# Strassen's scheme in the first MLP product of chunks 2 to 8 (three of four column groups), with in-place result sums and a new placement of attention

## The chip, the cores and the metric

The kernel runs on one core of a Trainium2 chip. The metric is the device time of one execution in microseconds (us). Times before and after are medians of several executions of the same rounds.

Engine names in the profile: PE is TensorE (matrix products), PEld its weight loads, DVE is VectorE, ACT is ScalarE, POOL is GpSimd, SP is the engine that issues most DMAs. PSUM holds the results of this kernel's matmuls, in buffers of two kinds, `ring` and `ops`; SBUF holds its other tiles.

## The reference

```python
def _attn_ref(q, k, v):                     # (8 batches, 8 heads, 576 positions, 64)
    q_s = np.exp(q - np.max(q, axis=-1, keepdims=True))
    q_s = q_s / (np.sum(q_s, axis=-1, keepdims=True) + 1e-09)
    k_s = np.exp(k - np.max(k, axis=2, keepdims=True))
    k_s = k_s / (np.sum(k_s, axis=2, keepdims=True) + 1e-09)
    kv = np.einsum('bhsd,bhse->bhde', k_s, v)
    return np.einsum('bhsd,bhde->bhse', q_s, kv)

def _moe_ref(x, w_in, w_out):               # x: 4608 x 512, w_in: 512 x 2048, w_out: 2048 x 512
    h = x @ w_in
    g = h * (1.0 / (1.0 + np.exp(-h)))      # SiLU
    return g @ w_out
# x is the attention output, heads side by side; result 4608 x 512, float32
```

## The kernel before

The 4608 rows are worked in nine chunks of 512 rows (0 to 8; the first product takes 576 of them in chunk 0 and 448 in chunk 1). A chunk has a first product (`mm1`, 512 x 512 by 512 x 2048), a SiLU on ScalarE, and a second product (2048 x 512), which runs interleaved with the first product of the next chunk. While chunk t is worked, the attention of batch t+1 is prepared: two exponentials on ScalarE, the row sums on VectorE, the scaling by their reciprocals and the cast of v on GpSimd (VectorE for batch 1), a transposing DMA, and two small products. In the timelines here, each engine executes its operations in the order in which the program issues them (one example, below: in chunk 4 of the changed kernel two sums run from 169.16 us on, ahead of an add at 172.68; in e1, which only issues those sums later, the add runs at 163.33 us and the sums behind it, at 169.01 and 171.00); the whole argument below turns on that order.

The second product of chunks 2 to 8 uses Strassen's scheme (Winograd's form): the matrix is halved in both directions, and seven products of quarters replace eight. The price is sums: `presum` builds the sums of activations on VectorE, and `after` combines the products from PSUM, also on VectorE. The first product is plain.

```python
def mm1(t, fb):                              # first product, one block of 128 columns
    for off, size in part[t]:
        hps = ps.tile([128, TCH], FP32, name="hps", tag="ring", bufs=PSB["ring"])
        for c in range(NC):                  # NC = 4: four matmuls of 512 moving columns
            nc.tensor.matmul(out=hps[:, 0:size], lhsT=W1[:, c, fb * 128:(fb + 1) * 128],
                             rhs=XT[t][:, c, off:off + size], start=(c == 0), stop=(c == NC - 1))
        # ... cut ...
            nc.scalar.activation(out=GT[g][:, fb, col:col + n], in_=hps[:, h], func=ACT.Silu)

def presum(t, i, f):                         # sums for the second product, f = half of the blocks
    S1, S2, S4 = SW[t % 2]
    V = nc.vector
    if i == 0:
        V.tensor_add(S1[:, f], quad(t, 0, f, 1), quad(t, 1, f, 1))
    elif i == 1:
        V.tensor_sub(S2[:, f], S1[:, f], quad(t, 0, f, 0))
    elif i == 2:
        V.tensor_sub(quad(t, 0, f, 1), quad(t, 0, f, 0), quad(t, 0, f, 1))
    else:
        V.tensor_sub(S4[:, f], quad(t, 1, f, 0), S2[:, f])

def plan_attn(b, u, sm, vs, tp, ks, ox, eng=nc.gpsimd):   # where attention of batch b stands
    for i, (x, y) in enumerate((("qt", "eq"), ("kt", "ek"))):
        plan(u + sm[i], lambda x=x, y=y: [exp(b, x, y, cc) for cc in range(2)])
    for cc in range(2):
        plan(u + sm[0] + 2 + 2 * cc, lambda cc=cc: (qsum(b, cc), qnorm(b, cc, nc.gpsimd)))
        plan(u + vs[cc], lambda cc=cc: vcast(b, cc, eng))
    plan(u + tp, lambda: tr_dma(b, nc.sync))
    # ... cut: loads of the next batch, the two small products ...
```

The softmax here doesn't subtract the row's maximum and nothing guards it: scores larger than these inputs give would overflow.

## Time and profile before

| | before |
|---|---|
| median time | 294.33 us (292.29 to 295.12, 4 runs) |
| span of the profiled run | 290.7 us |
| TensorE busy | 263.8 us (91%) |
| VectorE / ScalarE / GpSimd busy | 115.7 (40%) / 178.0 (61%) / 54.9 (19%) |

The first part of the page gives the busy time of each engine; the row "PEclk" of the second part gives the TensorE clock that was granted, in tenths of full speed, in 40 equal slices. Two lines of the page of before:

```profile
PE 263.8 (91%) x2269; PEld 162.4 (56%) x2306; DVE 115.7 (40%) x217; ACT 178.0 (61%) x287; POOL 54.9 (19%) x44
PEclk9999999999999999999999999999999999999999
```

TensorE bounds the kernel, and in this profiled run its clock does not fall (in later calls, runs of this kernel have mean clocks of 0.983 to 0.994). Of the view of TensorE's waits, the first two lines (total us, times, longest us): the copy `s` on ScalarE holds TensorE up four times, once in each of chunks 3 to 6.

```profile
PE ops L273 <- ACT s L295: 6.6, 4, 1.8
PE hps L206 <- ACT GT L220: 3.2, 2, 1.9
```

In TensorE's timeline of before (start, duration, line, operation, tiles, count; in brackets the idle time before it and what ended that), the wait of chunk 5 looks like this, and it is the only one above 0.3 us in its chunk:

```profile
169.66 1.03 PE L206 MATMUL hps<-XT,W 128*128 128x512 bf16 x4
172.27 1.03 PE L273 MATMUL ops<-W,GT 128*128 128x256 bf16 x8 [1.59 <-ACT s L295]
```

Chunk 0, where batch 1's inputs arrive: ScalarE's and SP's timelines of before.

```profile
30.23 0.88 ACT L220 ACTIVATE GT<-hps 128x320 bf16<-128x320 f32 x3 [0.96 <-PE hps L206]
31.82 1.28 ACT L91 ACT_TABLE_LOAD   x1 [0.70 <-DMA qt<-in_q_dram]
```

```profile
40.36 4.59 SPq L122 DMA_TRANSPOSE qT<-eq  x1
45.14 0.43 SPq L82 DMA_DIRECT2D qt<-in_q_dram  x1
```

The exponential waits only 0.70 us for its load, and the transposing DMA is issued ahead of the loads of the next batch. The second place is one that I read too late: VectorE's and GpSimd's timelines of before, in chunk 5.

```profile
175.63 0.69 DVE L231 TENSOR_TENSOR SW<-GT 128x1024 bf16<-128x1024 bf16 x1 [2.69 <-ACT GT L220]
176.36 1.52 DVE L233 TENSOR_TENSOR SW<-SW,GT 128x1024 bf16<-128x1024 bf16 x1
```

```profile
175.71 1.63 POOL L98 CAST vaug<-vt 128x1152 bf16<-128x1152 f32 x1
```

Two operations of the same shape take 0.69 and 1.52 us. The first began 0.08 us ahead of the GpSimd cast and kept its length, while the cast took 1.63 us instead of 1.16; the second began inside the cast and ended 0.54 us after it. Here nothing waits for it.

### The profile page before, as it was taken

To read this page: it belongs to the slowest core of one execution; us is meant where nothing else is said; L and a number is where in the kernel's file an instruction comes from. 1 tells how busy PE (TensorE), PEld (TensorE's weight loads), DVE (VectorE), ACT (ScalarE), POOL (GpSimd) and SP (SyncE) were. 2 spreads that over 40 slices of the span, in tenths; PEclk is the share of its full clock that TensorE was granted. 3 is DMA by queue.
4 is the path that set the end of the run, shared out by engine and by line. 5 is a ranking of instruction groups with operands and counts; after the bars stand their busy time and mean duration, and the time that the engine had idled before them with its cause. 6 is when DMAs were issued, how large, how long until landed. Compare 5 with 4: busy or idle time off the path is not lost.

```text
span 290.7 us, 5481 instructions
## 1 busy us (share of the span) xinstructions
PE 263.8 (91%) x2269; PEld 162.4 (56%) x2306; DVE 115.7 (40%) x217; ACT 178.0 (61%) x287; POOL 54.9 (19%) x44
## 2 busy tenths in 40 slices
PE   8589879995998997999799979997999999999993
PEld 3356544442443464656566656665656665665882
DVE  3830233841044335624562456245624041431621
ACT  4685794698797779356945594559545445544100
POOL 0661050035062007200630054004400000000000
PEclk9999999999999999999999999999999999999999
DMA  7799999966709920696049804971333012201234
GB/s 256 248 202 273 304 289 272 392 202 120 288 0 257 388 70 2 122 359 234 3 102 323 283 11 89 322 267 41 84 72 72 2 36 56 54 1 38 60 87 108
DMA packets 42377, 46.43 MB, mean 160 GB/s; under 512 B 18544, under 2 KB 29808, under 8 KB 42352
## 3 DMA queue, kind: packets, MB, share of 16 engines
q1 hardware_dynamic: 37312, 38.35, 44.1%
q0 software_dynamic: 5040, 7.73, 11.9%
q8 instruction: 18, 0.29, 0.4%
q14 instruction: 7, 0.06, 0.1%
HBM read 36.70 MB, written 9.44 MB: 159 GB/s over the span
## 4 chain that ended last, share of the span: by engine, by line
PE 54%; ACT 20%; DMA 18%; issue 3%; SPq 2%; POOL 2%; DVE 0%; ACTq 0%
PE ops L273 24%; PE hps L206 23%; DMA qt<-in_q_dram 8%; DMA out_dram<-oq 7%; ACT ek L91 5%; ACT L91 4%; ACT eq L91 4%; PE ops L331 3%; DMA vt<-in_v_dram 3%; ACT L220 3%; ACT GT L220 3%; PE kvps L153 2%; PE o L187 2%; SPq L122 1%; ACT s L295 1%
## 5 line engine op out<-in xcount | busy, mean ns | idle before, releaser
L206 PE MATMUL hps<-XT,W 128*128 128x512 bf16 (+3 forms) x612 | 139.2, 357 | 5.4 <-ACT GT L220 3.2
L220 ACT ACTIVATE GT<-hps 128x512 bf16<-128x512 f32 (+2 forms) x176 | 86.2, 523 | 77.3 <-PE hps L206 65.5
L206 PEld LDWEIGHTS <-W 128*128 128x128 bf16 x640 | 61.9, 98 | 52.4 <-issue 5.9
L111 POOL TENSOR_TENSOR eq<-eq,rzq 128x1152 bf16<-128x1152 bf16 x14 | 29.5, 2118 | 138.5 <-DVE rzq L106 138.5
L273 PEld LDWEIGHTS <-GT 128*128 128x128 bf16 x448 | 43.4, 98 | 22.0 <-issue 8.5
L105 DVE TENSOR_REDUCE zq<-eq 128x18 f32<-128x1152 bf16 x16 | 21.3, 1331 | 48.9 <-ACT eq L91 48.7
L273 PEld LDWEIGHTS <-SW 128*128 128x128 bf16 x336 | 31.9, 98 | 9.4 <-issue 0.8
L273 PE MATMUL ops<-W,GT 128*128 128x256 bf16 x224 | 28.7, 272 | 6.6 <-ACT s L295 6.6
L331 PE MATMUL ops<-W,GT 128*128 128x512 bf16 x120 | 31.5, 379 | 0.6 <-issue 0.2
L273 PE MATMUL ops<-TW,GT 128*128 128x256 bf16 x224 | 28.6, 273 | 0.4
L273 PE MATMUL ops<-TW,SW 128*128 128x256 bf16 x224 | 28.8, 273 | 0.0
L290 DVE SCALAR_TENSOR_TENSOR oq<-ops,u 128x512 f32<-128x512 f32 x14 | 9.7, 691 | 32.5 <-PE ops L273 32.5
L198 ACT CAST XT<-o 128x512 bf16<-128x512 f32 (+3 forms) x36 | 18.3, 564 | 5.1 <-PE o L187 5.1
L231 DVE TENSOR_TENSOR SW<-GT 128x1024 bf16<-128x1024 bf16 x14 | 9.6, 689 | 27.1 <-ACT GT L220 27.1
L91 ACT ACTIVATE eq<-qt 128x1152 bf16<-128x1152 f32 x16 | 17.9, 1157 | 3.0 <-DMA qt<-in_q_dram 2.9
L290 DVE SCALAR_TENSOR_TENSOR u<-ops,s 128x512 f32<-128x512 f32 x14 | 9.7, 692 | 23.4 <-PE ops L273 21.8
L331 PEld LDWEIGHTS <-GT 128*128 128x128 bf16 x128 | 12.1, 98 | 12.1 <-issue 0.7
L91 ACT ACTIVATE ek<-kt 128x1152 bf16<-128x1152 f32 x16 | 17.8, 1153 | 1.5 <-DMA kt<-in_k_dram 1.5
L98 POOL CAST vaug<-vt 128x1152 bf16<-128x1152 f32 x12 | 15.7, 1317 | 0.0
L220 ACT ACT_TABLE_LOAD x11 | 14.1, 1283 | 0.2
L273 PE MATMUL ops<-W,SW 128*128 128x256 bf16 x112 | 14.2, 273 | 0.0
L153 PE MATMUL kvps<-vaug,ek 64*64 64x65 bf16 x576 | 8.1, 194 | 6.4 <-ACT GT L220 2.8
(45 smaller groups left out, 140.9 us busy)
## 6 DMA issues: line engine op xcount, KB each, us to landing
qt<-in_q_dram SPq DMA_DIRECT2D x6, 1152.0 KB, 6.5
kt<-in_k_dram SPq DMA_DIRECT2D x6, 1152.0 KB, 9.4
vt<-in_v_dram SPq DMA_DIRECT2D x6, 1152.0 KB, 11.8
out_dram<-oq SPq DMA_DIRECT2D x42, 128.0 KB, 2.9
out_dram<-oq SPq DMA_DIRECT2D x60, 64.0 KB, 2.1
W<-in_moe_w_in_dram POOLq DMA_DIRECT2D x4, 512.0 KB, 9.9
W<-in_moe_w_out_dram POOLq DMA_DIRECT2D x4, 512.0 KB, 17.5
qt<-in_q_dram SPq DMA_DIRECT2D x2, 576.0 KB, 4.3
```

Source lines behind the costliest of these rows:

```text
L91: nc.scalar.activation(out=o, in_=jgd(st[b][src], cc), func=ACT.Exp)
L98: eng.tensor_copy(o, jgd(st[b]["vt"], cc))
L105: nc.vector.reduce_sum(out=st[b]["zq"][:, cc], in_=e, axis=AX.X)
L111: eng.tensor_tensor(out=e, in0=e, in1=r[:, :, :, None].to_broadcast([128, J, 2, D]), op=ALU.mult)
L153: nc.tensor.matmul(out=t[r][g * 64:(g + 1) * 64, 0:E1], lhsT=st[b]["ek"][r * P:(r + 1) * P, j, G * D:(G + 1) * D], rhs=vaug[b % 2][r * P:( ...
L198: nc.scalar.copy(out=x, in_=o1[g][:, 0:size])
L206: nc.tensor.matmul(out=hps[:, 0:size], lhsT=W1[:, c, fb * 128:(fb + 1) * 128], rhs=XT[t][:, c, off:off + size], start=(c == 0), stop=(c == ...
L220: nc.scalar.activation(out=GT[g][:, fb, col:col + n], in_=hps[:, h], func=ACT.Silu)
L231: V.tensor_add(S1[:, f], quad(t, 0, f, 1), quad(t, 1, f, 1))
L273: nc.tensor.matmul(out=o[:, a, :], lhsT=l(f), rhs=r(f), start=bool(first and a == 0 and f == 0), stop=(f == HF - 1), skip_group_check=True,)
L290: nc.vector.scalar_tensor_tensor(out=out, in0=o, scalar=1.0, in1=x, op0=ALU.mult, op1=ALU.add)
L331: nc.tensor.matmul(out=OP[t, tb], lhsT=GT[t][:, fc, tb * 128:(tb + 1) * 128], rhs=W2[:, fc, :], start=(fc == 0), stop=(fc == NFB - 1),)
```

## The change

The intent: the first product of chunks 2 to 8 gets the same scheme in three of its four groups of column blocks (group 0 stays plain, to give VectorE time to make the sums of the input). Seven products of 4 matmuls of 256 columns replace what were 16 matmuls of 512 columns per group. Results are summed in place to save buffers; PSUM is split 6 + 2 instead of 5 + 3; `vaug`, the tile for q and the sums SW become single-buffered; the positions of attention, of the sums and of the second product's pieces are written out anew for each chunk. The core of the diff, with lines left out:

```diff
-    vaug = [glob.tile([128, J, NG * E1], BF16, name=f"vaug{i}") for i in range(2)]
+    vaug = glob.tile([128, J, NG * E1], BF16, name="vaug")
-    LDB = {"qt": 2, "kt": 1, "vt": 1}
+    LDB = {"qt": 1, "kt": 1, "vt": 1}
+    def xsum(t, i):          # four sums of the chunk's input, VectorE
+    def vsum(i, k):          # eight sums of W1, VectorE, once
+    def product1(t, g, k):   # product k of group g: 2 x 2 matmuls of 256 columns, then
+        if k == 1:           # a copy s1 (ScalarE, for group 1 VectorE)
+        elif k == 6:
+            add(new("u2"), MP[t, g, "s1"])
+        elif k == 7:
+            add(new("u3"), MP[t, g, "s1"])
+        elif k == 2:
+            silu(o, 0, 0)
+        else:
+            x = MP[t, g, {5: "u3", 4: "s1", 3: "u2"}[k]]
+            add(x, x)                        # VectorE, from PSUM, in place
+            silu(x, *{5: (1, 1), 4: (1, 0), 3: (0, 1)}[k])
-    PSB = {"ring": 5, "ops": 3}
+    PSB = {"ring": 6, "ops": 2}
  ... cut ...
+    POS = {1: 0, 6: 1, 2: 3, 7: 4, 5: 5, 4: 6, 3: 9}     # order of the seven products in a group
+    def plan_attn(b, t, sm, qs, vs, tp, ks, ox, lq, lkv, eng=nc.gpsimd):
+        # sm: exponentials; qs: sums of q; vs: casts of v; tp: transpose;
+        # ks, ox: small products; lq, lkv: loads of the next batch. The loads of a position
+        # are now issued ahead of a transpose of the same position.
-    plan_attn(1, begin[1], (-18, -11), (-6, -5), -11, (-4, -3), (-2, 0), V)
+    plan_attn(1, 0, (6, 12), (8, 9), (11, 12), 12, (13, 14), (15, 16), 12, None, V)
+    plan_attn(2, 1, (5, 9), (7, 8), (9, 10), 10, (12, 13), (14, 15), 9, 11)
+    plan_attn(3, 2, (4, 8), (6, 8), (10, 12), 11, (16, 18), (21, 23), 10, 13)
     for b in range(4, B):
-        plan_attn(b, begin[b], (-25, -25), (-23, -21), -14, (-11, -9), (-5, -3))
+        plan_attn(b, b - 1, (1, 1), (4, 6), (6, 8), 10, (13, 16), (19, 21), 11, 12)
+            pre((t + 1, 6), 3, 0)            # the two sums S4 of the second product
+            pre((t + 1, 7), 3, 1)
```

More of the change, by code (lines that the diff above doesn't have):

```diff
@@ L54 @@
     TW = [glob.tile([128, HF, HM], BF16, name=f"TW{i}") for i in range(4)]
-    SW = [
-        [glob.tile([128, HF, 2, 128], BF16, name=f"SW{i}_{j}") for i in range(3)]
-        for j in range(2)
-    ]
-    vaug = [glob.tile([128, J, NG * E1], BF16, name=f"vaug{i}") for i in range(2)]
+    SW = [glob.tile([128, HF, 2, 128], BF16, name=f"SW{i}") for i in range(3)]
+    HT = TCH // 2
+    HK = NC // 2
+    F0 = 2
+    TX = [glob.tile([128, HK, (HF - F0) * 128], BF16, name=f"TX{i}") for i in range(4)]
+    XS = [glob.tile([128, HK, HT], BF16, name=f"XS{i}") for i in range(4)]
+    vaug = glob.tile([128, J, NG * E1], BF16, name="vaug")
     kvn = [glob.tile([128, 2, 2, D], BF16, name=f"kvn{i}") for i in range(3)]
@@ L93, in vcast @@
     def vcast(b, cc, eng):
-        o = vaug[b % 2].rearrange("p j (g e) -> p j g e", e=E1)[:, :, 2 * cc:2 * cc + 2, 0:D]
+        o = vaug.rearrange("p j (g e) -> p j g e", e=E1)[:, :, 2 * cc:2 * cc + 2, 0:D]
         if eng is nc.scalar:
@@ L155, in kv @@
                         lhsT=st[b]["ek"][r * P:(r + 1) * P, j, G * D:(G + 1) * D],
-                        rhs=vaug[b % 2][r * P:(r + 1) * P, j, G * E1:(G + 1) * E1],
+                        rhs=vaug[r * P:(r + 1) * P, j, G * E1:(G + 1) * E1],
                         start=(j == 0),
@@ L221, in mm1 @@
                 a += n
+    MP = {}
+    def xsum(t, i):
+        A = [[XT[t][:, k * HK:(k + 1) * HK, r * HT:(r + 1) * HT] for k in range(2)] for r in range(2)]
+        S1, S2, S3, S4 = XS
+        V = nc.vector
+        if i == 0:
+            V.tensor_add(S1, A[1][0], A[1][1])
+        elif i == 1:
+            V.tensor_sub(S2, S1, A[0][0])
+        elif i == 2:
+            V.tensor_sub(S3, A[0][0], A[1][0])
+        else:
+            V.tensor_sub(S4, A[0][1], S2)
+    def vsum(i, k):
+        c = lambda n: slice(n * HF * 128 + F0 * 128, (n + 1) * HF * 128)
+        B = [[W1[:, h * HK + k, c(n)] for n in range(2)] for h in range(2)]
+        T1, T2, T3, T4 = TX
+        o, a, b = (
+            (T1, B[0][1], B[0][0]),
+            (T2, B[1][1], T1[:, k]),
+            (T3, B[1][1], B[0][1]),
+            (T4, B[1][0], T2[:, k]),
+        )[i]
+        nc.vector.tensor_sub(o[:, k], a, b)
@@ new lines, in product1, with new, add, silu @@
+    def product1(t, g, k):
+        S1, S2, S3, S4 = XS
+        T1, T2, T3, T4 = TX
+        A = lambda r, h: (lambda c: XT[t][:, h * HK + c, r * HT:(r + 1) * HT])
+        S = lambda x: (lambda c: x[:, c, :])
+        B = lambda h, n: (
+            lambda c, f: W1[:, h * HK + c, (n * HF + f) * 128:(n * HF + f + 1) * 128]
+        )
+        T = lambda x: (lambda c, f: x[:, c, (f - F0) * 128:(f - F0 + 1) * 128])
+        bank, first, l, r = {
+            1: ("A", 1, B(0, 0), A(0, 0)),
+            2: ("A", 0, B(1, 0), A(0, 1)),
+            6: ("B", 1, T(T2), S(S2)),
+            7: ("B", 0, T(T3), S(S3)),
+            4: ("B", 0, T(T4), A(1, 1)),
+            5: ("C", 1, T(T1), S(S1)),
+            3: ("C", 0, B(1, 1), S(S4)),
+        }[k]
+        if first:
+            MP[t, g, bank] = ps.tile([128, 2, HT], FP32, name="hps", tag="ring", bufs=PSB["ring"])
+        o = MP[t, g, bank]
+        for f in range(2):
+            for c in range(HK):
+                nc.tensor.matmul(
+                    out=o[:, f, :],
+                    lhsT=l(c, 2 * g + f),
+                    rhs=r(c),
+                    start=bool(first and f == 0 and c == 0),
+                    stop=(c == HK - 1),
+                    skip_group_check=True,
+                )
+        def new(name):
+            MP[t, g, name] = mp.tile([128, 2, HT], FP32, name=name, tag="mt", bufs=6)
+            return MP[t, g, name]
+        def add(out, x):
+            nc.vector.scalar_tensor_tensor(
+                out=out, in0=o, scalar=1.0, in1=x, op0=ALU.mult, op1=ALU.add
+            )
+        def silu(x, r, n):
+            if t not in GT:
+                GT[t] = mp.tile([128, NFB, TCH], BF16, name="GT")
+            y = GT[t][:, n * HF + 2 * g:n * HF + 2 * g + 2, r * HT:(r + 1) * HT]
+            nc.scalar.activation(out=y, in_=x, func=ACT.Silu)
+        if k == 1:
+            if g in COPY_V:
+                nc.vector.tensor_scalar_mul(out=new("s1"), in0=o, scalar1=1.0)
+            else:
+                nc.scalar.activation(out=new("s1"), in_=o, func=ACT.Copy, scale=1.0)
+        elif k == 6:
[4 more added lines that the diff above has]
+            silu(o, 0, 0)
+        else:
+            x = MP[t, g, {5: "u3", 4: "s1", 3: "u2"}[k]]
+            add(x, x)
+            silu(x, *{5: (1, 1), 4: (1, 0), 3: (0, 1)}[k])
@@ L223, in quad @@
+    COPY_V = (1,)
     def quad(t, h, f, r):
@@ L227, in presum @@
     def presum(t, i, f):
-        S1, S2, S4 = SW[t % 2]
+        S1, S2, S4 = SW
         V = nc.vector
@@ L253, in product @@
     def product(t, k, a):
-        S1, S2, S4 = SW[t % 2]
+        S1, S2, S4 = SW
         T1, T2, T3, T4 = TW
@@ L284, in after, with new @@
     def after(t, k, o):
-        def new(name, bufs=1):
-            WP[t, name] = mp.tile([128, 2, HM], FP32, name=name, bufs=bufs)
+        def new(name):
+            WP[t, name] = mp.tile([128, 2, HM], FP32, name=name, tag="oq", bufs=6)
             return WP[t, name]
@@ L300, in after @@
         else:
-            q = new("oq", 4)
             if k == 2:
+                q = new("c11")
                 nc.scalar.activation(out=q, in_=o, func=ACT.Copy, scale=1.0)
             else:
-                add(q, WP[t, {5: "u3", 4: "s1", 3: "u2"}[k]])
+                q = WP[t, {5: "u3", 4: "s1", 3: "u2"}[k]]
+                add(q, q)
             qstore(t, q, *{2: (0, 0), 5: (1, 1), 4: (1, 0), 3: (0, 1)}[k])
@@ L326, in mm2 @@
         if qd == 0:
-            tag = "ops" if tb < 3 else "ring"
+            tag = "ops" if tb < 2 else "ring"
             OP[t, tb] = ps.tile([128, DM], FP32, name="ops", tag=tag, bufs=PSB[tag])
@@ L341, in store @@
     def store(t, tb, dve=0):
-        ost = mp.tile([128, DM], FP32, name="oq", bufs=4)
+        ost = mp.tile([128, DM], FP32, name="oq", tag="oq", bufs=6)
         if dve:
@@ L364 @@
     nc.vector.tensor_copy(ident, ident_f)
-    for t in vaug:
-        nc.vector.memset(t.rearrange("p j (g e) -> p (j g) e", e=E1)[:, :, D:E1], 1.0)
+    nc.vector.memset(vaug.rearrange("p j (g e) -> p (j g) e", e=E1)[:, :, D:E1], 1.0)
     FQ = DFF // 4
@@ L429, with xlist @@
     ORDER = (1, 6, 2, 7, 5, 4, 3)
-    xs = []
-    for t in range(NCH):
-        for i in range(NFB):
-            fb = i if t < STD else (i % 2) * HF + i // 2
-            xs.append((("mm1", t), lambda t=t, fb=fb: mm1(t, fb)))
-    behind = [[] for _ in range(len(xs) + 1)]
-    def trail(x, key, f):
-        behind[min(max(x, 0), len(xs) - 1)].append((key, f))
+    POS = {1: 0, 6: 1, 2: 3, 7: 4, 5: 5, 4: 6, 3: 9}
+    HALVES = [(m, a) for m in ORDER for a in range(2)]
+    def xlist(t):
+        if t < STD:
+            return [lambda fb=fb: mm1(t, fb) for fb in range(NFB)]
+        n = [lambda fb=fb: mm1(t, fb) for fb in (0, HF, 1, HF + 1)]
+        p = sorted((7 * g + POS[m], g, m) for g in range(1, HF // 2) for m in ORDER)
+        return n + [lambda g=g, m=m: product1(t, g, m) for _, g, m in p]
@@ L440, with trail @@
+    X = [xlist(t) for t in range(NCH)]
+    behind = {}
+    def trail(t, i, f):
+        behind.setdefault((t, i), []).append(f)
     for i in range(NFB):
-        trail(min(5 + i, NFB - 1), ("mm2", 0), lambda i=i: mm2(0, i))
+        trail(0, min(5 + i, NFB - 1), lambda i=i: mm2(0, i))
+    late = (0, 2, 4, 6, 9, 12, 15, 18, 21)
     for i in range(NFB):
-        trail(NFB + 6 + i * 3 // 2, ("mm2", 1), lambda i=i: mm2(1, i))
-    for t in range(STD, NCH):
-        for i, (m, a) in enumerate((m, a) for m in ORDER for a in range(2)):
-            late = 3 if t == NCH - 2 and i > 6 else 0
-            trail((t + 1) * NFB + 2 + i + late, ("mm2", t), lambda t=t, m=m, a=a: product(t, m, a))
@@ L448 @@
-    units = []
-    for i, x in enumerate(xs):
-        units.append(x)
-        units.extend(behind[i])
-    begin = {t: next(u for u, f in enumerate(units) if f[0] == ("mm1", t)) for t in range(NCH)}
-    index = [u for u, f in enumerate(units) if f[0][0] == "mm1"]
-    at = [[] for _ in units]
-    def plan(u, f):
-        at[u].append(f)
-    def plan_attn(b, u, sm, vs, tp, ks, ox, eng=nc.gpsimd):
+        if i < NFB - len(late):
+            trail(1, 6 + i * 3 // 2, lambda i=i: mm2(1, i))
+        else:
+            trail(2, late[i - NFB + len(late)], lambda i=i: mm2(1, i))
@@ new lines, with plan @@
+    YAT = (2, 3, 5, 7, 9, 11, 13, 15, 17, 19, 21, 23, 23, 23)
+    for t in range(STD, NCH - 1):
+        for i, (m, a) in enumerate(HALVES):
+            x = len(X[t + 1]) - 1 if t == NCH - 2 and i > 10 else YAT[i]
+            trail(t + 1, x, lambda t=t, m=m, a=a: product(t, m, a))
+    for m, a in HALVES:
+        X[NCH - 1].append(lambda m=m, a=a: product(NCH - 1, m, a))
+    NX = len(X[2])
+    at = {}
+    def plan(t, i, f):
+        at.setdefault((t, i), []).append(f)
+    def plan_attn(b, t, sm, qs, vs, tp, ks, ox, lq, lkv, eng=nc.gpsimd):
@@ L463, in plan_attn @@
         for i, (x, y) in enumerate((("qt", "eq"), ("kt", "ek"))):
-            plan(u + sm[i], lambda x=x, y=y: [exp(b, x, y, cc) for cc in range(2)])
+            plan(t, sm[i], lambda x=x, y=y: [exp(b, x, y, cc) for cc in range(2)])
         for cc in range(2):
-            plan(u + sm[0] + 2 + 2 * cc, lambda cc=cc: (qsum(b, cc), qnorm(b, cc, nc.gpsimd)))
-            plan(u + vs[cc], lambda cc=cc: vcast(b, cc, eng))
-        plan(u + tp, lambda: tr_dma(b, nc.sync))
-        if b == 1:
-            plan(u + vs[0] + 1, lambda: load_behind(2))
-        elif b + 1 < B:
-            plan(u + (tp - 5 if b == 2 else tp + 1), lambda: load(b + 1, "qt", q))
-            plan(max(u + tp, u + max(vs)) + 1, lambda: [load(b + 1, *y) for y in (("kt", k), ("vt", v))])
+            plan(t, qs[cc], lambda cc=cc: (qsum(b, cc), qnorm(b, cc, nc.gpsimd)))
@@ L474, in plan_attn @@
+            plan(t, vs[cc], lambda cc=cc: vcast(b, cc, eng))
+        if b + 1 < B:
+            if b == 1:
+                plan(t, lq, lambda: load_behind(2))
+            else:
+                plan(t, lq, lambda: load(b + 1, "qt", q))
+                plan(t, lkv, lambda: [load(b + 1, *y) for y in (("kt", k), ("vt", v))])
+        plan(t, tp, lambda: tr_dma(b, nc.sync))
         for cc in range(2):
-            plan(u + ks[cc], lambda cc=cc: kv(b, cc))
-            plan(u + ks[cc] + 1, lambda cc=cc: kvcopy(b, cc))
+            plan(t, ks[cc], lambda cc=cc: kv(b, cc))
+            plan(t, ks[cc], lambda cc=cc: kvcopy(b, cc))
@@ L477, in plan_attn @@
         for cc in range(2):
-            plan(u + ox[cc], lambda cc=cc: xt(b, cc))
+            plan(t, ox[cc], lambda cc=cc: xt(b, cc))
     def load_behind(b):
         st[b]["qt"] = ld.tile([128, NG, J * D], FP32, name="qt", bufs=LDB["qt"])
-        nc.vector.tensor_copy(st[b]["qt"][0:1, 0, 0:1], vaug[(b - 1) % 2][0:1, J - 1, D:E1])
+        nc.vector.tensor_copy(st[b]["qt"][0:1, 0, 0:1], vaug[0:1, J - 1, D:E1])
         for x in (("qt", q), ("kt", k), ("vt", v)):
@@ L487 @@
     V = nc.vector
-    plan_attn(1, begin[1], (-18, -11), (-6, -5), -11, (-4, -3), (-2, 0), V)
-    plan_attn(2, begin[2], (-16, -10), (-10, -9), -9, (-5, -4), (-3, -1))
-    plan_attn(3, begin[3], (-23, -17), (-17, -15), -15, (-10, -8), (-5, -3))
+    for i in range(8):
+        plan(1, i, lambda i=i: vsum(i // 2, i % 2))
+    for i in range(8):
+        plan(1, 8 + i, lambda i=i: wsum(i // 2, i % 2, V))
+    plan_attn(1, 0, (6, 12), (8, 9), (11, 12), 12, (13, 14), (15, 16), 12, None, V)
+    plan_attn(2, 1, (5, 9), (7, 8), (9, 10), 10, (12, 13), (14, 15), 9, 11)
@@ L491 @@
+    plan_attn(3, 2, (4, 8), (6, 8), (10, 12), 11, (16, 18), (21, 23), 10, 13)
     for b in range(4, B):
-        plan_attn(b, begin[b], (-25, -25), (-23, -21), -14, (-11, -9), (-5, -3))
+        plan_attn(b, b - 1, (1, 1), (4, 6), (6, 8), 10, (13, 16), (19, 21), 11, 12)
     for cc in range(2):
-        plan(begin[NCH - 1] - 7 + 3 * cc, lambda cc=cc: xt(NCH - 1, cc))
-    for i in range(8):
-        plan(index[NFB + i], lambda i=i: wsum(i // 2, i % 2, nc.vector))
+        plan(NCH - 2, 19 + 2 * cc, lambda cc=cc: xt(NCH - 1, cc))
@@ L498 @@
     for t in range(STD, NCH):
-        for h in range(2):
-            f = slice(h * HF // 2, (h + 1) * HF // 2)
-            for i in range(4):
-                x = t * NFB + 8 * (h + 1) + (i + 1) // 2
-                u = index[x] if x < len(index) else index[-1] + 1
-                plan(u, lambda t=t, i=i, f=f: presum(t, i, f))
-    for u, (_, f) in enumerate(units):
-        for g in at[u]:
+        for i, at_ in enumerate((0, 1, 2, 3)):
+            plan(t, at_, lambda t=t, i=i: xsum(t, i))
@@ new lines @@
+        fs = [slice(h * HF // 2, (h + 1) * HF // 2) for h in range(2)]
+        pre = lambda x, i, h: plan(*x, lambda t=t: presum(t, i, fs[h]))
+        pre((t, 21), 0, 0)
+        pre((t, 22), 1, 0)
+        pre((t, 23), 2, 0)
+        if t < NCH - 1:
+            pre((t + 1, 1), 0, 1)
+            pre((t + 1, 2), 1, 1)
+            pre((t + 1, 3), 2, 1)
+            pre((t + 1, 6), 3, 0)
+            pre((t + 1, 7), 3, 1)
+        else:
+            pre((t, NX), 0, 1)
+            pre((t, NX), 1, 1)
+            pre((t, NX), 2, 1)
+            pre((t, NX + 2), 3, 0)
+            pre((t, NX + 3), 3, 1)
@@ L508 @@
+    for t in range(NCH):
+        for i, f in enumerate(X[t]):
+            for g in at.pop((t, i), []):
+                g()
+            f()
+            for g in behind.pop((t, i), []):
+                g()
+        i += 1
+        for g in at.pop((t, i), []):
             g()
-        f()
+    assert not at and not behind
 _INS = ['q', 'k', 'v', 'moe_w_in', 'moe_w_out']
```

## The prediction

> **What bounds the kernel now.** TensorE. The page's first part has it busy 263.8 of 290.7 us; in the timeline chunks 4 to 6 repeat every 29.7 us, each with one idle gap of 1.6 us: product 2 waits for the ScalarE copy `s`, which stands behind table load and exponentials (waits view: 6.6 us over four such). VectorE is busy 40%, ScalarE 61%. The other TensorE gaps lie in chunks 0 to 2 (1.95, 1.27, 1.4 + 1.9, about 1.0 us).
>
> **Removed.** In the timeline, eight 256-column matmuls take 0.872 us and four 512-column ones 0.863 us: a column costs the same either way. A column group falls from 16 x 0.216 = 3.45 us to 28 x 0.109 = 3.05 us. Three groups in seven chunks: 21 x 0.40 = 8.4 us of TensorE, all on the critical path.
>
> **Added.** Per chunk, VectorE gets 15 adds from PSUM and one copy (0.69 us each), and four input sums of 512 elements (about 0.42 us, estimated from 0.69 us at 1024): 12 us more, so about 25 us of a 27 us chunk, in strict order. [...] ScalarE gets two copies (0.59 us each).
>
> **Moved, and where I expect loss.**
> 1. Chunk 0: batch 1's exponential of q now stands before column block 6 instead of behind block 9. That load lands at 31.8 us (chain of waits; ScalarE already waits 0.7 us for it), and the loads before it are unchanged. ScalarE would wait from about 23.5 us, TensorE run out of PSUM buffers in block 8 at about 28 and go on at about 37: a 9 us gap, for 1.95. Net about +6.5 us.
> 2. Chunk 0: batch 1's transposing DMA is now queued behind the three loads of batch 2 (3.5 MB). I estimate that it lands at 55 to 60 us; TensorE wants it at about 53: +2 to +6 us. [...]
> 3. Chunk 2: two separate exponential blocks stand before PSUM evacuations that the next group needs: about +3 us.
> 4. Chunks 3 to 6: group 1's fourth product waits for an add behind two reductions (1.35 us each) and two sums: a gap of about 2 us replaces that of 1.6 us. Each chunk 0.5 to 1 us shorter.
> 5. Chunks 7 and 8, without attention, keep their full 1.2 us each.
>
> Sum: +11 (0), +0.5 (1), +3 (2), -3 (3 to 6), -2.3 (7, 8) = +9 us.
>
> **Prediction: 303 us**, 291 to 311. Faster by over 2%: 0.09; within 2%: 0.22; slower by over 2%: 0.69.
>
> **What would show it.** TensorE's busy sum 7 to 9 us lower, yet the span longer; a long ScalarE wait for the q load at 24 to 32 us; chunk 1 starting at 59 to 66 us instead of 52; VectorE 60 to 65% busy; a gap of 1.5 to 2.5 us in each of chunks 3 to 6, released by VectorE; chunks 7 and 8 about 1.2 us shorter.
>
> **What would make it wrong.** The q load landing earlier; the transpose overtaking the loads; VectorE operations overlapping more closely than I assume, so that chunks 3 to 6 run without a gap (27 us each): then about 291 us.

Cut from the prediction: a term of chunk 0, +1 to +3 us for a lower clock behind its gaps. The sum, +11 for chunk 0 and +9 us in all (303 us), was made with that term; the terms of chunk 0 that are left, +6.5 and +2 to +6, come to 8.5 to 12.5 us.

## More of the kernel before

The experiments ran in four later calls, on four chips, and the kernel before was timed in each (medians 293.06 to 293.93 us), so a difference of about 1 us between runs of different calls says nothing; the ratios are free of this.

## The result, and the profile after

| | before | after |
|---|---|---|
| median time | 294.33 us (4 runs) | 331.82 us (331.18 to 332.97, 4 runs) |
| ratio | | 1.129, 95% interval 1.122 to 1.136 |
| span of the profiled run | 290.7 us | 329.4 us |
| mean granted clock | 1.0 | 0.933 |
| TensorE / VectorE busy | 263.8 / 115.7 us | 276.7 / 207.2 us |

Two lines of the page of after, and four of its view of TensorE's waits:

```profile
PE 276.7 (84%) x2558; PEld 193.9 (59%) x2558; DVE 207.2 (63%) x364; ACT 185.7 (56%) x301; POOL 57.0 (17%) x44
PEclk9999699699599989979996999599979999999999
```

```profile
PE hps L275 <- DVE u L289: 18.7, 11, 3.8
PE hps L208 <- ACT GT L222: 8.7, 1, 8.7
PE o L189 <- DMA qT<-eq: 7.4, 1, 7.4
PE hps L275 <- ACT s L303: 3.5, 1, 3.5
```

The clock row now has dips in every chunk from 0 to 6. TensorE's busy sum went up although there is less to multiply, since matmuls at the lower clock count longer (four of 256 columns 1.01 us instead of 0.60, below).

Chunk lengths, from the start of the first matmul of a chunk to that of the next in TensorE's timeline:

| chunk | before | after | difference | predicted |
|---|---|---|---|---|
| 0 (to its end) | 52.1 | 68.1 | +16.0 | +11 |
| 1 | 24.1 | 26.9 | +2.8 | +0.5 |
| 2 | 25.3 | 31.5 | +6.2 | +3 |
| 3, 4, 5, 6 | 29.7, 29.7, 29.7, 29.7 | 33.3, 33.9, 34.0, 32.4 | +14.8 | -3 |
| 7 | 26.9 | 25.8 | -1.1 | -1.2 |
| 8 and tail | 43.3 | 43.3 | 0.0 | -1.2 |

The largest error is in chunks 3 to 6. TensorE's timeline of after in chunk 4, where product 4 of group 1 (the sixth in the order) accumulates into the PSUM buffer that product 7 filled, and so waits until VectorE has read product 7 out of it:

```profile
169.04 0.60 PE L275 MATMUL hps<-XS,TX 128*128 128x256 bf16 x4
173.41 1.01 PE L275 MATMUL hps<-XT,TX 128*128 128x256 bf16 x4 [3.76 <-DVE u L289]
174.21 1.91 PE L367 MATMUL ops<-W,GT 128*128 128x256 bf16 x8
```

Before the gap four matmuls of 256 columns show 0.60 us, behind it 1.01; eight show 1.91 instead of 1.03. The clock has fallen. The trace's record of the clock has it at half for 3.4 us in chunk 3, 6.8 us in chunks 4 and 5 and 3.4 us in chunk 6. VectorE's and GpSimd's timelines of after in the same moments:

```profile
167.60 1.34 DVE L107 TENSOR_REDUCE zq<-eq 128x18 f32<-128x1152 bf16 x1
168.97 0.27 DVE L108 RECIPROCAL rzq<-zq 128x18 f32<-128x18 f32 x1
169.16 3.59 DVE L331 TENSOR_TENSOR SW<-GT,SW 128x1024 bf16<-128x1024 bf16 x2
172.68 0.68 DVE L289 SCALAR_TENSOR_TENSOR u<-hps,s 128x512 f32<-128x512 f32 x1
```

```profile
168.54 1.15 POOL L100 CAST vaug<-vt 128x1152 bf16<-128x1152 f32 x1
169.65 2.55 POOL L113 TENSOR_TENSOR eq<-eq,rzq 128x1152 bf16<-128x1152 bf16 x1
172.15 1.61 POOL L100 CAST vaug<-vt 128x1152 bf16<-128x1152 f32 x1
```

The two sums S4 (line 331) took 3.59 us together, and they stood directly ahead of the add `u` that TensorE waited for. GpSimd was at work all that time.

In chunk 0, ScalarE's, TensorE's and SP's timelines of after show the two gaps that the prediction named, with larger numbers:

```profile
30.56 1.28 ACT L93 ACT_TABLE_LOAD   x1 [7.98 <-DMA qt<-in_q_dram]
```

```profile
35.87 1.01 PE L208 MATMUL hps<-XT,W 128*128 128x256 bf16 x4 [8.68 <-ACT GT L222]
59.58 0.59 PE L189 MATMUL o<-qT,kvn 64*64 64x448 bf16 x4 [7.37 <-DMA qT<-eq]
```

```profile
42.90 0.37 SPq L84 DMA_DIRECT2D qt<-in_q_dram  x1
48.63 8.85 SPq L124 DMA_TRANSPOSE qT<-eq  x1
```

Before, chunk 0's two largest gaps were 1.95 and 1.27 us. The two new ones are 12.8 us longer. The transpose was late mainly by order: its input was ready at about 39.5 us (e4, below), but ahead of it in SP's queue stood the load of k, whose buffer became free only at 47.66 us. The other 3.2 of the 16.0 us I put down to the half clock behind each gap (an estimate, by subtraction).

### The profile page after: what moved, and what is told of

It reads as the page before. It is cut to its first block, busy times and chain, and to the rows that moved or that the text cites. A ratio compares the mean times of both kernels' runs of the same rounds, so it can differ in the third digit from the quotient of the medians.

```text
span 329.4 us, 6236 instructions
## 1 busy us (share of the span) xinstructions
PE 276.7 (84%) x2558; PEld 193.9 (59%) x2558; DVE 207.2 (63%) x364; ACT 185.7 (56%) x301; POOL 57.0 (17%) x44
## 4 chain that ended last, share of the span: by engine, by line
PE 54%; ACT 15%; DVE 13%; DMA 9%; issue 6%; POOL 1%; SPq 0%; DVEq 0%; POOLq 0%; ACTq 0%
PE ops L367 22%; PE hps L275 15%; PE hps L208 7%; PE ops L426 5%; DMA qt<-in_q_dram 5%; DVE SW L331 4%; ACT L93 4%; DMA qT<-eq 3%; ACT eq L93 3%; DVE u L289 3%; DVE zq L107 2%; ACT ek L93 2%; ACT GT L222 2%; PE o L189 2%; PE kvps L155 2%
## 5 line engine op out<-in xcount | busy, mean ns | idle before, releaser
L208 PE MATMUL hps<-XT,W 128*128 128x512 bf16 (+3 forms) x304 | 61.3, 346 | 9.7 <-ACT GT L222 8.7
L297 ACT ACTIVATE GT<-u 128x512 bf16<-128x512 f32 x42 | 26.5, 630 | 53.4 <-DVE u L289 53.3
L275 PEld LDWEIGHTS <-TX 128*128 128x128 bf16 x336 | 32.8, 101 | 27.2 <-issue 20.9
L289 DVE SCALAR_TENSOR_TENSOR u<-hps,s 128x512 f32<-128x512 f32 x42 | 28.9, 688 | 30.5 <-ACT s L303 14.9
L222 ACT ACTIVATE GT<-hps 128x512 bf16<-128x512 f32 (+4 forms) x92 | 36.3, 458 | 17.0 <-PE hps L208 16.5
L275 PE MATMUL hps<-XS,TX 128*128 128x256 bf16 x252 | 38.2, 281 | 1.5 <-DVE u L289 0.8
L289 DVE SCALAR_TENSOR_TENSOR u<-hps,u 128x512 f32<-128x512 f32 x42 | 28.7, 683 | 5.6 <-PE hps L275 4.6
L275 PE MATMUL hps<-XT,W 128*128 128x256 bf16 x168 | 26.7, 284 | 3.5 <-ACT s L303 3.5
L367 PE MATMUL ops<-TW,SW 128*128 128x256 bf16 x224 | 28.8, 273 | 0.0
L367 PE MATMUL ops<-TW,GT 128*128 128x256 bf16 x224 | 28.7, 273 | 0.0
L275 PE MATMUL hps<-XT,TX 128*128 128x256 bf16 x84 | 14.0, 295 | 16.7 <-DVE u L289 16.6
L426 PEld LDWEIGHTS <-GT 128*128 128x128 bf16 x128 | 13.4, 104 | 12.8 <-issue 2.9
L297 ACT ACTIVATE GT<-s 128x512 bf16<-128x512 f32 x21 | 13.2, 629 | 12.4 <-DVE s L289 12.4
```

The lines of the kernel that those rows point to most:

```text
L275: nc.tensor.matmul(out=o[:, f, :], lhsT=l(c, 2 * g + f), rhs=r(c), start=bool(first and f == 0 and c == 0), stop=(c == HK - 1), skip_group ...
L289: nc.vector.scalar_tensor_tensor(out=out, in0=o, scalar=1.0, in1=x, op0=ALU.mult, op1=ALU.add)
L297: nc.scalar.activation(out=y, in_=x, func=ACT.Silu)
L367: nc.tensor.matmul(out=o[:, a, :], lhsT=l(f), rhs=r(f), start=bool(first and a == 0 and f == 0), stop=(f == HF - 1), skip_group_check=True,)
L426: nc.tensor.matmul(out=OP[t, tb], lhsT=GT[t][:, fc, tb * 128:(tb + 1) * 128], rhs=W2[:, fc, :], start=(fc == 0), stop=(fc == NFB - 1),)
```

## The experiments

The order theory: in chunks 3 to 6 the sums S4 are placed wrongly, ahead of an add that TensorE waits for. Within it, the neighbour theory: the sums are slow because GpSimd works at the same time. The load rival: VectorE has simply too much to do (63% busy over the span, more in a chunk), and any order would leave such a gap. (The letters A to G in the expectations name theories of one run or a few each; a letter can change its meaning from one run to the next.) For chunk 0, two faults, the early exponential and the late transpose, which either add or overlap. All diffs are against the changed kernel unless another is named.

### e1: the two S4 sums later

```diff
-            pre((t + 1, 6), 3, 0)
-            pre((t + 1, 7), 3, 1)
+            pre((t + 1, 12), 3, 0)
+            pre((t + 1, 14), 3, 1)
```

> Changed kernel with one move: the two halves of the fourth activation sum (S4 of the second product) stand at chunk positions 12 and 14 instead of 6 and 7, so behind the add that releases TensorE. Theory A (order on VectorE: the sums stand ahead of that add, are slowed beside GpSimd, and the gap they make also lowers the clock): the 3.8 us gap in chunks 3 to 6 falls below 1 us, the clock there stays at 1.00, chunks 4 and 5 fall from 34.0 us to 27.5 to 29 us, total 331.8 to about 308 to 313. Theory B (VectorE has too much work altogether, the in-place sums and its 26.4 us per chunk set the pace): the wait turns up elsewhere in the chunk, chunks 4 and 5 stay above 32 us, total above 323.

Measured: 311.95 us, ratio 1.061 (1.055 to 1.068). Two lines moved, and 19.9 us came back. Chunks 4 and 5 take 28.8 us each; chunks 3 to 6 together are 3.3 us shorter than before. That this is near the -3 that I had predicted for them is chance, since e1 is not the order that I had predicted for; e2 is the fair test of that term. TensorE's timeline of e1 at the same place:

```profile
164.01 0.60 PE L275 MATMUL hps<-XT,TX 128*128 128x256 bf16 x4 [0.20 <-DVE u L289]
165.35 1.03 PE L367 MATMUL ops<-W,GT 128*128 128x256 bf16 x8 [0.74 <-ACT s L389]
```

The gap of 3.76 us is 0.20, the clock stays up (0.60 us for the four matmuls behind it, 1.03 for the next eight), and a new, smaller wait on ScalarE appears. VectorE's work is the same, so the load rival falls as the cause of this gap. GpSimd's multiplications and casts now show 2.12 and 1.16 us, and each of the S4 sums 0.68 us: once apart, nobody is slowed. VectorE's and GpSimd's timelines of e1:

```profile
169.01 0.68 DVE L331 TENSOR_TENSOR SW<-GT,SW 128x1024 bf16<-128x1024 bf16 x1
171.00 0.68 DVE L331 TENSOR_TENSOR SW<-GT,SW 128x1024 bf16<-128x1024 bf16 x1
```

```profile
163.82 2.12 POOL L113 TENSOR_TENSOR eq<-eq,rzq 128x1152 bf16<-128x1152 bf16 x1
165.88 1.16 POOL L100 CAST vaug<-vt 128x1152 bf16<-128x1152 f32 x1
```

### e2: GpSimd idle (a wrong result on purpose)

```diff
-            plan(t, qs[cc], lambda cc=cc: (qsum(b, cc), qnorm(b, cc, nc.gpsimd)))
-            plan(t, vs[cc], lambda cc=cc: vcast(b, cc, eng))
+            plan(t, qs[cc], lambda cc=cc: (qsum(b, cc), b < 4 and qnorm(b, cc, nc.gpsimd)))
+            plan(t, vs[cc], lambda cc=cc: b < 4 and vcast(b, cc, eng))
```

> Wrong result on purpose: changed kernel without GpSimd's work (scaling of q, cast of v) for batches 4 to 7, VectorE's order as it was. Theory A (the pair of sums takes 3.6 us instead of 1.3 because GpSimd works in SBUF beside it): the pair takes 1.3 to 1.4 us, the gap falls from 3.8 to about 1.5 us, no fall of the clock, chunks 4 and 5 about 28 to 29 us. Theory C (the pair is slow by itself, by its access pattern or a wait): it still takes about 3.6 us and the chunks stay at 34 us.

Measured: 312.61 us, ratio 1.064 (1.059 to 1.069). The order is that of the changed kernel; only GpSimd's scaling and casts are gone from batch 4 on. VectorE's and TensorE's timelines of e2:

```profile
165.32 1.22 DVE L331 TENSOR_TENSOR SW<-GT,SW 128x1024 bf16<-128x1024 bf16 x2
```

```profile
167.20 0.60 PE L275 MATMUL hps<-XT,TX 128*128 128x256 bf16 x4 [1.39 <-DVE u L289]
```

1.22 us instead of 3.59, and the gap falls from 3.76 to 1.39 us, without a fall of the clock (0.60 us for the four matmuls behind it; chunks 4 and 5: 28.8 and 28.7 us; chunks 3 to 6 together 3.5 us shorter than before). So the extra 2.37 us of the pair come from GpSimd's work at the same time, and the neighbour theory is shown. By what means GpSimd's work slows them, the runs do not show. In the trace of after, the first sum began at 169.16 inside a cast that ended at 169.69 and took 1.07 us, the second began at 170.15 inside the multiplication that ended at 172.20 and took 2.60 us, GpSimd's next two operations were lengthened by 0.43 and 0.46 us (2.55 and 1.61 instead of 2.12 and 1.15), and VectorE's reduction (one input, 1.34 us) and its add from PSUM (0.68 us) beside GpSimd were not lengthened (1.34 and 0.68 us in e2 as well).

### e3: the gap filled with idle matmuls

Sixteen matmuls into a PSUM buffer that nothing reads stand in the gap of chunks 3 to 6, so that TensorE has work while it would wait.

```diff
+    def fill(n):
+        w = ps.tile([128, 512], FP32, name="wfill", tag="ring", bufs=PSB["ring"])
+        for _ in range(n):
+            nc.tensor.matmul(out=w, lhsT=warm[:, 0:128], rhs=warm, start=True, stop=True)
+    for t in range(3, 7):
+        plan(t, 9, lambda: fill(16))
```

> Changed kernel with 16 dummy matmuls (3.45 us, on zeros) in front of the delayed fourth product of group 1 in chunks 3 to 6, so that TensorE is busy in the gap. Theory A (the idle gap lowers the clock): the wait for VectorE ends as before, but the matmuls after it run at full rate: chunks 4 and 5 fall by 2.5 to 3 us to about 31 us, total down by 8 to 11 us. Theory D (the matmuls after the gap are slow for another reason, such as contention): nothing gained, or a loss, chunks at 34 us or more.

Measured: 322.99 us, ratio 1.099 (1.095 to 1.103), 8.8 us less than the changed kernel by adding work that does nothing. TensorE's timeline of e3:

```profile
168.11 3.61 PE L623 MATMUL wfill<-warm 128*128 128x512 bf16 x16
171.81 0.60 PE L275 MATMUL hps<-XT,TX 128*128 128x256 bf16 x4
172.25 1.04 PE L367 MATMUL ops<-W,GT 128*128 128x256 bf16 x8
```

Product 4 starts 13.50 us after the start of its chunk, in this kernel (158.31 to 171.81) as in the changed one (159.91 to 173.41). The wait is as long as it was, but the matmuls behind it run at full rate, and the chunk takes 31.15 us instead of 33.94. So 2.8 us of this chunk is the clock alone. In chunks 3 to 6 it is 1.7, 2.8, 2.9 and 1.3 us, 8.6 us together, in step with the 3.4 and 6.8 us for which the clock was at half. Behind the gap in after, the matmuls of 256 columns start 0.213 us apart instead of 0.109. The fall itself came at 172.33 us there, 2.69 us after the gap began.

### e4 and e5: the two faults of chunk 0, one at a time

e4 puts the loads of batch 2 behind the transpose; e5 puts batch 1's exponentials and sums later and leaves the loads ahead of the transpose.

```diff
 # e4
-    plan_attn(1, 0, (6, 12), (8, 9), (11, 12), 12, (13, 14), (15, 16), 12, None, V)
+    plan_attn(1, 0, (6, 12), (8, 9), (11, 12), 12, (13, 14), (15, 16), 13, None, V)
 # e5
+    plan_attn(1, 0, (10, 13), (10, 11), (11, 12), 12, (13, 14), (15, 16), 12, None, V)
```

> Changed kernel with one move in chunk 0: the loads of batch 2 are issued at position 13, behind the transposing DMA of batch 1, not ahead of it. Theory A: the transpose lands at about 47 us instead of 59.5, the 7.4 us wait for it goes, with the slower matmuls behind it; chunk 1 starts at 58 to 60 us instead of 68.1; total down by 8 to 10 us. Theory E (the transpose is late because VectorE and GpSimd prepare its input late): the wait stays within 2 us of 7.4.

> Changed kernel with the exponentials of batch 1 in chunk 0 put back to where they stood before (behind column block 9, and behind block 12 for k), the loads of batch 2 still ahead of the transpose. Theory A (two faults in a row: the early exponential holds TensorE at 27 to 36 us, and the transpose behind the loads holds it again at 52 to 59.5 us): the 8.7 us gap falls to about 2 us with no fall of the clock there, but TensorE only waits longer for the transpose, which lands 2 to 5 us earlier than 59.5; chunk 1 starts at 63 to 66 us instead of 68.1, total down by only 2 to 5 us. Theory F (the losses of the two gaps simply add): total down by 8 to 9 us.

Measured: e4 322.95 us, ratio 1.099 (1.093 to 1.105); e5 331.38 us, ratio 1.131 (1.128 to 1.134), no gain at all. SP's timelines of e4 and of e5, and TensorE's of e5:

```profile
39.53 4.62 SPq L124 DMA_TRANSPOSE qT<-eq  x1
```

```profile
45.77 11.31 SPq L124 DMA_TRANSPOSE qT<-eq  x1
```

```profile
59.26 0.59 PE L189 MATMUL o<-qT,kvn 64*64 64x448 bf16 x4 [12.26 <-DMA qT<-eq]
```

In e4 the wait for the transpose is gone and chunk 1 starts at 60.5 us instead of 68.1. In e5 the first gap falls from 8.68 us to 1.26, with a new one of 2.19 beside it, but the product that needs the transpose starts at 59.26 us, as before at 59.58: what the one gap gave up, the other took (12.26 instead of 7.37 us). The transpose was issued 2.9 us earlier than in the changed kernel and its issue took 2.5 us longer; in both it landed 2.0 to 2.2 us after the load of v ahead of it (57.42 and 59.44 us in after, 56.97 and 59.13 in e5). The transpose is the later of two things to be waited for, so the exponential's fault can cost nothing more while the transpose's stands. My expectation of 2 to 5 us for e5 was wrong.

### e7: all three moves

The S4 sums of e1, the later exponentials of e5 and the order of e4.

```diff
-    plan_attn(1, 0, (6, 12), (8, 9), (11, 12), 12, (13, 14), (15, 16), 12, None, V)
+    plan_attn(1, 0, (10, 13), (10, 11), (11, 12), 12, (13, 14), (15, 16), 13, None, V)
 # and e1
```

> All three moves: the sums late, the exponentials of chunk 0 late, the transpose ahead of the loads. Theory A: chunk 1 starts at 52 to 53 us as before the change; chunks 4 and 5 take 28.8 us; total 294 to 298, so level with the kernel before, the rest of the Strassen gain lost in chunks 1 and 2 (together about 8 us longer than before the change). Theory B (VectorE work sets the pace): total above 303.

Measured: 304.94 us, ratio 1.041 (1.034 to 1.048): less than expected. The positions of the sums of q and of the casts of v put one cast between the two sums on VectorE, and that cast waits for v's load; so the transpose was issued only at 45.90 us, and chunk 1 started at 59.3 us instead of 52 to 53. The total lies above the 303 us that the expectation had named as the mark of its theory B; but chunks 4 and 5 take the 28.8 us of its theory A, and the excess is in chunks 0 to 2. SP's and TensorE's timelines of e7:

```profile
45.90 2.81 SPq L124 DMA_TRANSPOSE qT<-eq  x1
```

```profile
50.74 0.46 PE L189 MATMUL o<-qT,kvn 64*64 64x448 bf16 x4 [3.61 <-DMA qT<-eq]
```

### e8 and e9: chunks 2 and 1 placed anew

e8 is e7 with both exponential blocks of chunk 2 at its start and the last pieces of chunk 1's second product earlier; e9 is e8 with chunk 1 reordered.

```diff
 # e8, on e7
-    plan_attn(3, 2, (4, 8), (6, 8), (10, 12), 11, (16, 18), (21, 23), 10, 13)
+    plan_attn(3, 2, (1, 1), (4, 6), (6, 8), 11, (16, 18), (21, 23), 12, 13)
-    late = (0, 2, 4, 6, 9, 12, 15, 18, 21)
+    late = (0, 0, 0, 1, 1, 2, 2, 3, 3)
 # e9, on e8
-            trail(1, 6 + i * 3 // 2, lambda i=i: mm2(1, i))
+            trail(1, (6, 7, 8, 9, 11, 13, 15)[i], lambda i=i: mm2(1, i))
-    plan_attn(2, 1, (5, 9), (7, 8), (9, 10), 10, (12, 13), (14, 15), 9, 11)
+    plan_attn(2, 1, (6, 6), (8, 9), (4, 5), 11, (13, 14), (15, 16), 12, 12)
```

> The three moves, and chunk 2 rearranged: one block of exponentials at position 1 instead of two at 4 and 8, and the nine remaining row-block products of chunk 1 all in positions 0 to 3, so that TensorE works through that block and the two PSUM buffers that they hold come free early. Theory A (chunk 2 lost 6.2 us to evacuations behind the two exponential blocks, and to the clock after the 3.5 us gap): chunk 2 falls from 30 us to 24 to 26 us, total 288 to 292. Theory G (the PSUM ring is too small for three banks per group whatever the order): chunk 2 stays above 28 us.

> As the last, and chunk 1 rearranged: one block of exponentials at position 6, four row-block products of chunk 1 right behind it, v cast by GpSimd ahead of the scaling of q. Theory A (chunk 1 loses time to two exponential blocks and to the late cast of v): chunk 1 falls from about 26 to 22 or 24 us, total 285 to 289. If the single block overfills the PSUM ring, chunk 1 stays at 26 us or more and the total does not change.

Measured: e8 303.14 us, ratio 1.035 (1.027 to 1.042); e9 298.83 us, ratio 1.020 (1.016 to 1.023). e8 missed by far, with 29.4 us for chunk 2 instead of 24 to 26: the sums of q queued on VectorE behind the copies of chunk 1's output, so the first product of chunk 2 waited 2.08 us for its copy `s`, and then 1.07 us for an add. e9 got what was expected of chunk 1 (22.4 us instead of 26.9), and missed the total through the same waits in chunk 2. These waits show something of the clock. TensorE's timelines of e8 and of e9 at the same instruction:

```profile
103.75 0.60 PE L275 MATMUL hps<-XT,TX 128*128 128x256 bf16 x4 [1.07 <-DVE u L289]
```

```profile
99.05 1.01 PE L275 MATMUL hps<-XT,TX 128*128 128x256 bf16 x4 [1.07 <-DVE u L289]
```

The same two gaps, 2.08 and 1.07 us, came about 3 us apart in both; in e9 the clock fell, in e8 it did not. In e9 it was at half from 97.87 us on (eight matmuls from 96.95 us on still show 1.03 us, the four behind the second gap 1.01), before the second gap began at 97.98 us, so that gap did not lower it. The length of a gap alone does not decide either: the same wait of 3.50 us in chunk 2 was followed by a fall in the profiled runs of after, e2, e3, e4 and e7 (chunk 2: 31.5 us), and by none in those of e1 and e5 (30.5 us). In the trace of after, all falls and rises between 32.39 and 244.01 us lie whole multiples of 3.413 us apart, and a stretch at half lasts 3.41 or 6.83 us. What decides whether a gap is followed by a fall, these runs do not show.

### e11 and e12: the order repaired everywhere, with the scheme and without it

e11 adds to e9 a chunk 0 with its casts and small products among the last column blocks (the loads stay behind the transpose), and chunk 2 with the sums of q at its start. e12 is e11 with the first product plain: in the same positions, each group runs its four column blocks with 512-column matmuls, and the sums of x and W1 are not made.

```diff
 # e11, on e9
-    plan_attn(1, 0, (10, 13), (10, 11), (11, 12), 12, (13, 14), (15, 16), 13, None, V)
+    plan_attn(1, 0, (10, 13), (11, 12), (15, 15), 13, None, None, 15, None, V)
+    # kv, kvcopy and xt of batch 1 among the last pieces of chunk 0's second product
-    plan_attn(3, 2, (1, 1), (4, 6), (6, 8), 11, (16, 18), (21, 23), 12, 13)
+    plan_attn(3, 2, (1, 1), (1, 1), (4, 5), 11, (16, 18), (21, 23), 12, 13)
 # e12, on e11: in product1
+        if k in (1, 2, 5, 4):
+            mm1(t, 2 * g + {1: 0, 2: HF, 5: 1, 4: HF + 1}[k])
+        return
 # e12: xsum and vsum return at once
```

> Everything so far, and two repairs more. In chunk 0 the products of k and v of batch 1, and with them the cast of v, go back among the last row-block products, where they stood before the change, so that the reductions for q are not held up by the cast and the transpose starts at about 40 us instead of 46. In chunk 2 the two reductions stand directly behind the first input sum, ahead of the copies of the output. Theory A (all that is lost is order): chunk 1 starts at 52 to 53 us, chunk 2 takes 24 to 26 us without a fall of the clock, total 284 to 289, faster than the kernel before by 1.5 to 3%. Theory B (the in-place scheme costs VectorE so much that it cannot win): no better than 293.

> The last kernel without what the change was made for: the first product of chunks 2 to 8 again as plain 512-column products in the same positions, its input and weight sums left out, all else as in the last. It measures what Strassen's scheme is worth where the order costs nothing. Expected: TensorE work 8.4 us more than in the last kernel; in chunks 3 to 6 a part of that comes back, since waits of about 1.1 us per chunk for VectorE and ScalarE may shrink. Total 4 to 8 us longer than the last kernel, so about 290 to 296. If the scheme were worthless even so (rival), the two differ by less than 2 us.

Measured: e11 288.23 us (6 runs), ratio 0.983 (0.980 to 0.986). e12 283.72 us (6 runs), ratio 0.967 (0.962 to 0.971), so 4.5 us shorter than e11 where I expected 4 to 8 us longer. The repaired order beats the kernel before, and in that order the scheme makes it worse. One chunk of each, the view of busy time by window (window, length, then busy us and count for PE, PEld, DVE, ACT, POOL, then clock, DMA share and GB/s), first e12, then e11:

```profile
155.77:184.06 28.29, 27.87 (x261) 17.90 (x264) 14.02 (x25) 18.93 (x28) 6.39 (x4) 1.00 0.61 185
```

```profile
159.26:188.04 28.78, 27.45 (x302) 21.42 (x301) 23.82 (x46) 19.93 (x30) 6.40 (x4) 1.00 0.63 181
```

VectorE goes from 14.0 to 23.8 us in a chunk of 28 us. TensorE's waits, two lines of e11 and one of e12:

```profile
PE hps L275 <- DVE u L289: 3.0, 12, 0.6
PE ops L367 <- ACT s L389: 3.0, 4, 0.7
```

```profile
PE ops L372 <- ACT s L394: 0.6, 4, 0.2
```

In a steady chunk, 1.2 us are saved by the scheme, and about 2.0 us of e11 against 0.3 of e12 are lost between the starts of neighbouring matmuls, so the chunk is 0.5 us longer. Chunks 2 and 3 together are 5.0 us longer (57.4 against 52.4), with 4.6 us of listed waits against 0.2; I have not assigned each of these. Chunk 2 of e11 took 28.1 us, where I had expected 24 to 26; e12's took 23.9. VectorE was busy in it for only 14.2 us, so its load alone is not the reason there. That three PSUM buffers per group are too many for the ring, which is theory G in e8's expectation, stays a rival: its mark, a chunk 2 above 28 us, was met in e8, e9 and e11 (29.4, 31.4 and 28.1 us), and no run changed the ring. Chunk 7, which has no attention, is 1.19 us shorter with the scheme (25.74 against 26.93). Chunk 0 ended 2.0 us later in e12's profiled run, where the granted clock has a dip in its third slice (14 to 21 us) that e11's has not (48 matmuls of 320 columns from 16.88 us on show 7.62 us, in e11 6.05); that is no effect of the scheme, which chunk 0 does not use.

### e13 and e14: the scheme in chunks 7 and 8 alone

That left a version to try: the scheme where VectorE has room. e13 is e12 with it in the last two chunks; e14 is e12 once more, for a comparison in the same rounds.

```diff
 # e13, on e11
+        if t < 7:            # in product1; xsum returns likewise
+            if k in (1, 2, 5, 4):
+                mm1(t, 2 * g + {1: 0, 2: HF, 5: 1, 4: HF + 1}[k])
+            return
-        plan(1, i, lambda i=i: vsum(i // 2, i % 2))
+        plan(5, 8 + i, lambda i=i: vsum(i // 2, i % 2))
```

> The repaired order with plain 512-column matmuls in chunks 2 to 6 and Strassen's scheme in chunks 7 and 8 alone, which have no attention; the sums of W1 are made in chunk 5. If the scheme costs time only where VectorE and ScalarE have attention to do: chunk 7 takes 25.7 us instead of 26.9, chunk 8 with the tail 43.2 instead of 43.4, chunks 4 to 6 stay at 28.3 each, and the median is 1.2 to 1.5 us below that of the plain order in the same call (about 282.3 us against 283.7). Rival, that the scheme pays nowhere here: the same time within 0.4 us, or longer.

> The repaired order with plain matmuls in every chunk, once more, so that it and the kernel with the scheme in the last two chunks are timed in one call on one chip. 283 to 285 us; chunks 4 to 6 at 28.3 us each, chunk 7 at 26.9.

Measured: e13 282.21 us (281.5 to 282.9, 5 runs), ratio 0.961 (0.959 to 0.963); e14 283.73 us (282.73 to 284.11, 5 runs), ratio 0.965 (0.963 to 0.968). As expected, 1.5 us apart: chunk 7 takes 25.74 us in e13 and 26.93 in e14, chunk 8 with the tail 43.20 and 43.45, chunks 4 to 6 28.3 in both. Before chunk 4 both stand at the same time (126.73 and 126.80 us). TensorE's waits in e13 from chunk 7 to the end have one entry:

```profile
PE hps L281 <- DVE u L295: 0.6, 1, 0.6
```

That is 0.6 of the 0.95 us that chunk 8 lacks of its full 1.2. e13 is the fastest kernel, 4% below the kernel before; nearly nine tenths of that (3.5 of 3.9%) came without the scheme. This part is the new order together with the changed buffers (PSUM split 6 + 2, single-buffered tiles, sums in place), which are in e12 to e14 too; no run separates the two.

## Why the prediction was right or wrong

The direction was right (slower), and so were the mechanisms named for chunk 0 and the wait in chunks 3 to 6; for chunk 2 that is shown only in part (with one exponential block, in e8, the wait of 3.50 us was gone, but the chunk fell only from 31.5 to 29.4 us). The size was wrong: 303 us predicted, range 291 to 311, measured 331.8. Step by step:

- **The step that failed** is number 4: "group 1's fourth product waits for an add behind two reductions (1.35 us each) and two sums: a gap of about 2 us replaces that of 1.6 us. Each chunk 0.5 to 1 us shorter." (It is product 4, sixth in the order.) The releaser and the queue ahead of it were right. The cost of the two sums was wrong, and with it the size of the gap. The gap measured 3.76 us, since the two sums took 3.59 us beside GpSimd where they take 1.22 without it (e2), and behind a gap of that length the clock was low, for another 1.3 to 2.9 us in each chunk, 8.6 us in the four (e3). The term was -3 us; it measured +14.8. In the order predicted, but with GpSimd idle, it is -3.5 (e2), with a gap of 1.39 us: four gaps longer by 2.37 us, 9.5 us, and the clock's 8.6 make up 18.1 of the difference of 18.3 us. I had taken 0.68 us for such a sum as a fixed duration; the trace of before already held a sum of the same shape at 1.52 us beside a GpSimd cast.
- **Chunk 0** was +11, measured +16.0. The first gap was expected at 9 and measured 8.68. The wait for the transpose was expected at 2 to 6 and measured 7.37; it landed at 59.4, inside my 55 to 60. The rest I put down to the clock behind both gaps (3.2 us, an estimate, by subtraction); the 1 to 3 us that I had allowed for it is the term that is cut.
- **Chunk 1** was +0.5, measured +2.8. Its two waits, for GpSimd's cast of v and for ScalarE, grew by 0.5 us, from 1.37 + 1.86 to 2.64 + 1.10 us; the rest I put down to the clock, which had not fallen there before (mean 1.00) and was at half for 6.8 us now (mean 0.87; an estimate, by subtraction). **Chunk 2** was +3, measured +6.2: waits of 1.55, 3.50, 0.62 and 0.66 us, again on queues of VectorE and ScalarE, and about 1 us of clock (31.5 us, against 30.5 in e1 and e5 with the same waits and no fall). e9 and e11 show that placement alone moves chunk 1 (22.4 us).
- **"8.4 us of TensorE, all on the critical path."** The size per chunk is right where nothing else is in the way: 1.19 us in chunk 7. In the chunks with attention it is not. With the order repaired, the scheme in chunks 2 to 6 costs more than it saves (e11 against e12; in chunks 4 to 6 by 0.5 us each). "Added" was costed well (VectorE 63% against 60 to 65% predicted), but the sum of busy times said that it fits, and the question was in which order it is ready.
- **TensorE's busy sum 7 to 9 us lower** did not come: it is 12.9 us higher; the fall of the clock lengthens matmuls (1.01 us for four of 256 columns instead of 0.60). Yet in e11 too, at a mean clock of 0.996, it is 262.3 us, only 1.5 below that of before: the busy sum was a poor sign to look for.
- **Chunks 7 and 8**: -1.1 for chunk 7, against -1.2 predicted; chunk 8 gave nothing (43.3 us both times; one wait of 0.6 us is listed, the rest is not assigned).
- The 0.69 us for an add from PSUM was right: 0.68 us for 512 elements with a PSUM operand, as against 0.68 us for 1024 bf16 elements from SBUF, in the traces of before, after and e1. But I did not ask what a neighbour does to them: for two-input sums from SBUF this duration was measured where they ran alone (1.22 us for two in e2), not beside GpSimd (3.59 us in after).

What stays open: why e11's chunks 2 and 3 lose 5.0 us to e12's in detail, whether the size of the PSUM ring has a part in it, what of the 3.5% is due to the changed buffers, and whether an order exists in which the scheme pays in the chunks with attention. I tried one.

## What to carry to other kernels

Costs of operations are not enough when an engine runs in program order: ask, for each result that the bounding engine waits for, what stands ahead of it in the queue, and whether that can be slowed by a neighbour (here two two-input VectorE sums, 3.59 us beside GpSimd and 1.22 without). A gap on TensorE that grows from 1.4 to 3.8 us can cost more than its length, through the clock: all twelve gaps of 3.8 us in the profiled runs of after, e4 and e5 were followed by a fall, and none of the gaps of 1.4 us in chunks 3 to 6 of e2. And when a change brings both a new algorithm and a new order, test the order without the algorithm: here the order, with the buffers that came with it, was worth 3.5% and the algorithm only the last 0.5%, in the two chunks that had room for it.
